# Loading the first q and k of an attention-and-experts kernel in fp32 by a hardware queue, and turning them on TensorE in fp32

## The chip, the cores and the metric

The kernel runs on one core of a Trainium2 chip. The metric is the device time of one execution in microseconds (us). The kernel before takes 1054.22 us, the median of 3 runs (1053.27 to 1054.75).

## The reference, cut to what matters

There are two parts. The first is a linear attention over 8 batches, 8 heads, 576 positions and 64 channels; its features are exponentials of a small projection, scaled by a row maximum. The second is a dense mixture of 8 experts over its output, weighted by an iterated normalisation of the routing table.

```python
def phi(x):                                   # x is q or k, per batch and head
    proj = np.einsum('bhsd,df->bhsf', x, w_phi)
    proj = proj - np.max(np.abs(proj), axis=-1, keepdims=True)
    return np.concatenate([np.exp(proj), np.exp(-proj)], axis=-1)
q_p, k_p = phi(q), phi(k)
kv = np.einsum('bhsf,bhsd->bhfd', k_p, v)     # then num / den, and out is x of the experts
...
logits = x @ w_gate                           # 4608 x 512 @ 512 x 8
...                                           # 8 normalisations of rows and columns
for e in range(8):
    out += P[:, e:e+1] * (np.maximum(x @ w1[e], 0.0) @ w2[e])
```

## The kernel before

The attention goes by pairs of heads: pair i is heads 2p and 2p+1 of batch i // 4, with p = i % 4, so there are 32 pairs (0 to 31). 512 of a head's 576 positions are the main part; the 64 that are left of all heads are the "rests", one block a batch. Matmuls of expert 0 are mixed into the attention to fill TensorE. Every operation is put in a list, and a scheduler in the program, with its own estimates of durations, fixes each engine's order when the kernel is built. On the chip each engine works in that order: an operation that has to wait holds up all that stand behind it on its engine.

The parts that the change touches (cut):

```python
def load_qk(b, hh, nh, t, r=()):              # q and k of nh heads: GpSimd queue, fp32 to bf16 on the way
    ...
    for x, src in ((1, k), (0, q)):
        dma("POOL", nh << 17, 230, lambda x=x, src=src: nc.gpsimd.dma_start(
            out=t["qk"]()[:, x, o:o + nh],
            in_=src[b, hh:hh + nh, 0:SM].rearrange("h (p j) d -> p h (j d)", j=NJ)),
            r, [(t["qk"], x, i) for i in keys])

def pair_a(b, pr, t):                         # for batches 0 and 1: TensorE turns q and k
    ...
    if b < 2:
        for x in (1, 0):
            ptr = new("P1")
            for c in range(4):
                pe(128, lambda x=x, c=c, ptr=ptr: nc.tensor.transpose(
                    bf(ptr)[:, c * 128:(c + 1) * 128],
                    t["qk"]()[:, x, h0 + c // 2, (c % 2) * 128:(c % 2) * 128 + 128],
                    ident), [(t["qk"], x, h0 // 2), "ident"], [ptr])
            dve(256, lambda x=x, ptr=ptr: nc.vector.tensor_copy(   # PSUM to SBUF, VectorE
                out=t["T"]()[:, x, 2 * h0:2 * h0 + 4, :].rearrange("p a b -> p (a b)"),
                in_=bf(ptr)[:, 0:512]), [ptr], [(t["T"], x, h0 // 2)])
    ...                                       # projections, maxima, exponentials;
    # then GpSimd multiplies v by the exponentials of the maxima ("the v product")

# start of the program
load_qk(0, 0, 2, halves[0, 0])                # pair 0
...                                           # w_phi on the SyncE queue
load_v(0, 0, 2, halves[0, 0])
pool(300, lambda: make_identity(nc, ident), w=["ident"])
...
load_rests(0, 1)                              # rests of batch 0: 4 issues on GpSimd's queue
load_qk(0, 2, 2, halves[0, 0])                # pair 1
load_v(0, 2, 2, halves[0, 0])
load_qk(0, 4, 4, halves[0, 1])                # pairs 2 and 3
load_v(0, 4, 4, halves[0, 1])
...
dma("POOL", 1 << 14, 50, lambda: nc.gpsimd.dma_start(      # gate weights, cast on the way
    out=wgate, in_=moe_w_gate.rearrange("(c p) e -> p c e", p=128)), w=["wgate"])

def stage_a(i):                               # for each pair, as it is put in the list
    b, pr = i // 4, i % 4
    st[i] = pair_a(b, pr, halves[b, pr // 2])
    if pr == 0:
        rs[b] = rest_a(b, rests[b])
    gt = [("max", 0, i - 1)] if i >= 1 else []             # loads of the next batch wait for this
    if b + 1 < B and pr in (0, 2):
        ...
        load_qk(b + 1, 2 * pr, 4, t, gt)
        load_v(b + 1, 2 * pr, 4, t, gt)
        if b + 1 >= 2:
            turn_qk(t)                        # from batch 2 on the DMA engines turn q and k
    ...
```

`acc` are the fp32 accumulators of the experts (five tiles of 128 x 4 x 512), idle in the first two batches.

## Time and profile before

| | before |
|---|---|
| time, median of 3 | 1054.22 us |
| span in the profile | 1054.0 us |
| TensorE busy | 1022.4 us, 97% |
| TensorE idle in the first 80 us | 20.2 us |
| VectorE, ScalarE, GpSimd busy | 824.6, 707.8, 475.4 us |

The first view is the profile's page: busy time and number of instructions of each engine, then the busy tenths of the span in 40 slices of 26 us (PEclk is TensorE's granted clock), then the DMA queues (packets, MB, share of the engines' time).

```profile
span 1054.0 us, 24517 instructions
...
PE 1022.4 (97%) x9512; PEld 841.3 (80%) x9512; DVE 824.6 (78%) x1634; ACT 707.8 (67%) x1560; POOL 475.4 (45%) x551
...
PE   5889999999899999999999999999999999999998
...
PEclk9899999999999999999999999999999999999999
...
q1 hardware_dynamic: 65040, 63.78, 22.3%
q0 software_dynamic: 40080, 26.23, 18.2%
...
```

TensorE (PE) is full from the fourth slice on, so only its first three slices, about 80 us, have anything to give. Of the two DMA queues, q0 is GpSimd's, which casts on the way; q1 is the hardware queue.

The next view cuts the start into stretches. After the bounds and length of a stretch stand, for each engine, the busy us and the number of instructions, then TensorE's granted clock, the DMA share and the rate.

```profile
...
core 0: us, PE busy (x) PEld busy (x) DVE busy (x) ACT busy (x) POOL busy (x), PEclk, DMA share, GB/s
0.00:5.00 5.00, 0.43 (x4) 0.35 (x4) 2.57 (x8) 1.28 (x1) 3.86 (x11) 1.00 0.49 99
5.00:10.00 5.00, 3.67 (x16) 1.42 (x14) 3.33 (x6) 2.66 (x8) 5.00 (x8) 1.00 1.35 251
10.00:15.00 5.00, 3.16 (x20) 2.23 (x21) 1.93 (x4) 2.94 (x9) 3.15 (x6) 1.00 1.52 174
15.00:20.00 5.00, 3.67 (x30) 2.31 (x29) 4.26 (x10) 5.00 (x16) 4.76 (x10) 1.00 0.86 103
20.00:25.00 5.00, 3.58 (x70) 2.90 (x70) 2.71 (x8) 1.56 (x4) 4.92 (x10) 1.00 0.26 46
25.00:30.00 5.00, 4.21 (x28) 2.56 (x26) 4.87 (x15) 4.46 (x11) 2.04 (x6) 0.57 1.34 214
...
```

Adding TensorE's busy time of the stretches up to 80 us gives 59.8 us, hence 20.2 us idle. GpSimd (POOL) is busy 4.76 and 4.92 us of 5 at 15 to 25 us. The clock of 0.57 in the last row shown is half speed for most of that stretch.

TensorE's list of waits (what was waited for, then us in total, times, longest) names two loads:

```profile
...
PE P_144 L457 <- DMA qk<-in_k_dram: 4.6, 1, 4.6
PE P_214 L395 <- DMA qk_r<-in_q_dram: 2.4, 1, 2.4
...
```

And this is the chain of waits that ended last, in order of time (start, duration, what):

```profile
...
1.26 0.48 POOL qk L324
...
3.57 1.79 POOL qk_r L367 x3
5.36 6.26 DMA qk_r<-in_q_dram
...
11.75 0.60 PE P_214 L395 x4
...
18.37 0.26 POOL vrd_88 L440
...
18.85 0.60 POOL vrd_89 L440
...
```

The rests' loads (qk_r) are issued by GpSimd from 3.57 us on and hold TensorE until 11.75 us; pair 1 stands behind them. At 18.37 to 20.5 us the chain is GpSimd's own products.

### The profile page before, as it was taken

What the parts mean: (1) busy time and instruction counts of PE and PEld (TensorE: products, weight loads), DVE (VectorE), ACT (ScalarE), POOL (GpSimd) and SP (SyncE); (2) the same over time, 40 slices, a digit from 0 to 9 for tenths busy, and PEclk for the clock granted to TensorE, in tenths of its full rate; (3) what the DMA queues carried; (4) which work ended last, traced back from release to release, by engine and by line L of the source; (5) the groups of instructions that cost most, each with busy time, mean ns of one, the idle gap of its engine ahead of it and who ended that gap; (6) DMA issues with size and microseconds to landing.
All of it is one profiled execution on the core that took longest, in us unless ns stands there. A gap on an engine that the chain in (4) does not pass through costs nothing.

```text
span 1054.0 us, 24517 instructions
## 1 busy us (share of the span) xinstructions
PE 1022.4 (97%) x9512; PEld 841.3 (80%) x9512; DVE 824.6 (78%) x1634; ACT 707.8 (67%) x1560; POOL 475.4 (45%) x551
## 2 busy tenths in 40 slices
PE   5889999999899999999999999999999999999998
PEld 3546666654588888888888888888888888888886
DVE  6889988988867787778877787778777877777775
ACT  5789989954896656666666666665666666666663
POOL 8776755510044344334444444444333544434442
PEclk9899999999999999999999999999999999999999
DMA  9998886914511133113411341116111521114333
GB/s 143 141 187 133 136 142 121 159 47 164 101 41 47 48 89 81 41 51 81 89 43 41 76 86 42 49 46 127 41 41 51 111 61 42 41 41 128 114 131 120
DMA packets 105236, 91.57 MB, mean 87 GB/s; under 512 B 45344, under 2 KB 80288, under 8 KB 105120
## 3 DMA queue, kind: packets, MB, share of 16 engines
q1 hardware_dynamic: 65040, 63.78, 22.3%
q0 software_dynamic: 40080, 26.23, 18.2%
q8 instruction: 74, 1.21, 0.5%
q14 instruction: 42, 0.34, 0.1%
HBM read 94.98 MB, written 14.16 MB: 104 GB/s over the span
## 4 chain that ended last, share of the span: by engine, by line
PE 89%; ACT 4%; DVE 3%; DMA 2%; POOL 1%; issue 1%; DVEq 0%; ACTq 0%; POOLq 0%
DVE m L376 1%; DMA qkT<-qk 1%; ACT U L1027 1%; DMA qk_r<-in_q_dram 1%; DVE xb L590 0%; PE P_13550 L999 0%; PE P_12438 L999 0%; PE P_8591 L999 0%; PE P_15513 L999 0%; PE P_14556 L999 0%; PE P_14095 L999 0%; PE P_13743 L999 0%; PE P_13392 L999 0%; PE P_13188 L999 0%; PE P_12788 L999 0%
## 5 line engine op out<-in xcount | busy, mean ns | idle before, releaser
L999 PEld LDWEIGHTS <-S 128*128 128x128 bf16 x1984 | 194.1, 98 | 22.9 <-issue 0.5
L999 PEld LDWEIGHTS <-T 128*128 128x128 bf16 x1512 | 147.9, 98 | 20.4 <-issue 3.2
L999 PEld LDWEIGHTS <-hT 128*128 128x128 bf16 x1488 | 145.6, 98 | 16.9
L907 DVE TENSOR_TENSOR S<-hT 128x1024 bf16<-128x1024 bf16 x124 | 80.3, 684 | 0.0
L1155 POOL TENSOR_TENSOR acc_77<-acc_77,V 128x512 f32<-128x512 f32 x28 | 36.3, 1308 | 54.6 <-ACT V L1152 54.5
L1155 POOL TENSOR_TENSOR acc_78<-acc_78,V 128x512 f32<-128x512 f32 x28 | 37.4, 1349 | 49.0 <-ACT V L1152 48.9
L1155 POOL TENSOR_TENSOR acc_81<-acc_81,V 128x512 f32<-128x512 f32 x28 | 35.6, 1276 | 51.0 <-ACT V L1152 50.5
L1155 POOL TENSOR_TENSOR acc_4738<-acc_4738,V 128x512 f32<-128x512 f32 x28 | 35.5, 1274 | 51.1 <-ACT V L1152 50.5
L1155 POOL TENSOR_TENSOR acc_4740<-acc_4740,V 128x512 f32<-128x512 f32 x28 | 35.2, 1268 | 51.3 <-ACT V L1152 51.2
L1155 POOL TENSOR_TENSOR acc_80<-acc_80,V 128x512 f32<-128x512 f32 x28 | 35.4, 1269 | 49.9 <-ACT V L1152 49.3
L1155 POOL TENSOR_TENSOR acc_4737<-acc_4737,V 128x512 f32<-128x512 f32 x28 | 35.6, 1277 | 49.0 <-ACT V L1152 48.4
L1155 POOL TENSOR_TENSOR acc_79<-acc_79,V 128x512 f32<-128x512 f32 x28 | 35.8, 1289 | 48.1 <-ACT V L1152 47.6
L384 PEld LDWEIGHTS <-hT 128*128 128x128 bf16 x320 | 30.7, 101 | 26.6 <-issue 2.2
L1155 POOL TENSOR_TENSOR acc_4739<-acc_4739,V 128x512 f32<-128x512 f32 x24 | 30.4, 1273 | 37.3 <-ACT V L1152 36.9
L384 PEld LDWEIGHTS <-w_449 128*128 128x128 bf16 x288 | 26.1, 98 | 24.0 <-issue 2.9
L907 DVE TENSOR_TENSOR S<-S,hT 128x1024 bf16<-128x1024 bf16 x62 | 42.5, 685 | 0.8
L907 DVE TENSOR_TENSOR S<-hT,S 128x1024 bf16<-128x1024 bf16 x62 | 42.3, 682 | 0.0
L384 PEld LDWEIGHTS <-qkT 128*128 128x128 bf16 x256 | 24.4, 102 | 20.6 <-DVE xb_r L595 4.4
L999 PEld LDWEIGHTS <-w_3831 128*128 128x128 bf16 x288 | 28.2, 98 | 4.2 <-issue 0.7
L999 PEld LDWEIGHTS <-w_13099 128*128 128x128 bf16 x288 | 28.2, 98 | 3.3
L999 PEld LDWEIGHTS <-w_11515 128*128 128x128 bf16 x288 | 28.2, 98 | 3.3
L999 PEld LDWEIGHTS <-w_5153 128*128 128x128 bf16 x288 | 28.2, 98 | 3.3
(4017 smaller groups left out, 3296.2 us busy)
## 6 DMA issues: line engine op xcount, KB each, us to landing
v_m<-in_v_dram SPq DMA_DIRECT2D x15, 512.0 KB, 5.4
qk<-in_k_dram POOLq DMA_DIRECT2D x15, 256.0 KB, 5.1
qk<-in_q_dram POOLq DMA_DIRECT2D x15, 256.0 KB, 5.8
X<-xd_98 SPq DMA_DIRECT2D x7, 256.0 KB, 2.6
X<-xd_99 SPq DMA_DIRECT2D x7, 256.0 KB, 2.7
X<-xd_100 SPq DMA_DIRECT2D x7, 256.0 KB, 2.7
X<-xd_101 SPq DMA_DIRECT2D x7, 256.0 KB, 3.1
X<-xd_102 SPq DMA_DIRECT2D x7, 256.0 KB, 2.6
```

The source lines that it names most:

```text
L376: dve(el, lambda: nc.vector.tensor_reduce(out=dst(), in_=src(), axis=AX.X, op=ALU.max, apply_absolute_value=True), r, w)
L384: nc.tensor.matmul(out_, lhsT=lhsT, rhs=rhs, start=start, stop=stop)
L907: lambda: f.tensor_tensor(out=out_(), in0=x(), in1=y(), op=op), r, w, **kw)
L999: pe(256, lambda i=i, k=k, z=z: nc.tensor.matmul(bank()[:, 256 * i:256 * i + 256], lhsT=lhs(k, i), rhs=rhs(k), start=first and z, stop=k = ...
L1027: act(512, lambda: nc.scalar.copy(out=u[fp][n]().rearrange("p a b -> p (a b)"), in_=x[fp]()), [x[fp]], [u[fp][n]])
L1155: pool(670, lambda: nc.gpsimd.tensor_tensor(out=acc[g][:, 2 * i:2 * i + 2, 256 * j:256 * j + 256], in0=acc[g][:, 2 * i:2 * i + 2, 256 * j: ...
```

## The change

Its intent: take the loads of q, k and rests of batches 0 and 1 and of the gate weights off GpSimd's queue, whose issues take GpSimd 0.6 to 0.85 us each, and start pairs 0 and 1 sooner. On the hardware queue they are loaded without a cast, so q and k land in fp32, in the idle accumulators. TensorE turns them in fp32. VectorE copies the turned k and ScalarE the turned q to bf16. The loads of batch 0's rests go behind those of pair 1. The gate weights land in fp32 and ScalarE casts them. Two more things move: the two loads of w_phi (the weights of the projection) go from SyncE's queue to ScalarE's, and the identity matrix for the turns is made in fp32 and cast to bf16 by ScalarE. As the list of operations is new, the scheduler also fixes a new order. The diff, cut to its core (the rest is dead code taken out, which leaves the operations as they were):

```diff
 def load_qk(...):
+        if b < 2:
+            g = t["f"]
+            for x, src in ((1, k), (0, q)):
+                i = 2 * x + o // 2
+                dma("SP", nh << 17, 320, lambda x=x, src=src, i=i: nc.sync.dma_start(
+                    out=acc[g][:, i:i + nh // 2].rearrange("p a (h c) -> p (a h) c", h=2),
+                    in_=src[b, hh:hh + nh, 0:SM].rearrange("h (p j) d -> p h (j d)", j=NJ)),
+                    r, [("acc", g, 2 * x + n) for n in keys])
+            return
 ...                                        # load_rests: the same, into acc[0]; rest_a: fp32 turns
 def pair_a(...):
-                    pe(128, lambda x=x, c=c, ptr=ptr: nc.tensor.transpose(
-                        bf(ptr)[:, c * 128:(c + 1) * 128],
-                        t["qk"]()[:, x, h0 + c // 2, (c % 2) * 128:(c % 2) * 128 + 128],
-                        ident), [(t["qk"], x, h0 // 2), "ident"], [ptr])
-                dve(256, ...)
+                    pe(128, lambda c=c, i=i, ptr=ptr: nc.tensor.transpose(
+                        ptr()[:, c * 128:(c + 1) * 128], acc[g][:, i, c * 128:c * 128 + 128],
+                        identf), [("acc", g, i), "identf"], [ptr])
+                if x:
+                    dve(512, lambda x=x, ptr=ptr: nc.vector.tensor_copy(...
+                else:
+                    act(512, lambda x=x, ptr=ptr: nc.scalar.copy(...
 ...                                        # w_phi's two loads: nc.sync to nc.scalar
-    pool(300, lambda: make_identity(nc, ident), w=["ident"])
+    pool(300, lambda: make_identity(nc, identf), w=["identf"])
+    act(128, lambda: nc.scalar.copy(out=ident, in_=identf), ["identf"], ["ident"])
 ...
+    load_qk(0, 2, 2, halves[0, 0])
     load_rests(0, 1)
-    load_qk(0, 2, 2, halves[0, 0])
 ...
-    dma("POOL", 1 << 14, 50, lambda: nc.gpsimd.dma_start(
-        out=wgate, in_=moe_w_gate.rearrange("(c p) e -> p c e", p=128)), w=["wgate"])
+    dma("SP", 1 << 14, 50, lambda: nc.sync.dma_start(
+        out=wgate_f, in_=moe_w_gate.rearrange("(c p) e -> p c e", p=128)), w=["wgate_f"])
+    act(32, lambda: nc.scalar.copy(out=wgate, in_=wgate_f), ["wgate_f"], ["wgate"])
```

## The prediction

> **What bounds the kernel now.** The page gives a span of 1054.0 us with TensorE busy 97%: from about 80 us on it is TensorE-bound. The change touches only the first two batches, so it can gain only what TensorE loses in the first 80 us. The table by stretches shows TensorE idle there for 20.2 us, partly at a reduced clock (0.57 and 0.75 at 25-35 us). Three causes:
> - The start. In the list of waits TensorE waits 4.6 us for the first k and 2.4 us for the first rests, behind which pair 1 stands (its turn starts at 12.1 us). DMA share is over 1 at 5-15 us, at only 174-251 GB/s.
> - GpSimd. It issues 19 loads of q, k, rests and gate weights, 0.62 to 0.85 us each, about 14 us, between its products. It is busy 4.8 to 4.9 us of each 5 at 15-25 us; the chain of waits runs through it at 18.4-22.9 us, with VectorE idle (2.7 of 5 busy).
> - VectorE. It is full (4.8 to 5.0 of 5) at 25-45 us, which sets about 6.4 us a pair.
>
> **Removed, added, moved.**
> - Loads: the GpSimd queue loses 19 issues. The first k issues at about 0.75 instead of 1.26 us and lands about 3.8 instead of 4.57 us (256 KB on the hardware queue took 3.6 us at the median). Pair 1, queued before the rests, should be ready at 7 to 8.5 us instead of 12. Products on GpSimd start 3 to 5 us earlier.
> - TensorE: 72 transposes become fp32. The trace has fp32 weight loads (routing): 190 ns against 98 for bf16. The Trainium skill, "TensorE: Matmul & The Clock Gate" (Weight-path perf modes), says fast weight load is off for FP32; the trace agrees in direction. I take one pass per transpose, about 0.8 us per group of four instead of 0.22 to 0.43: 18 groups, about +8 us of TensorE, mostly where it idles; perhaps 1.5 us of it in latency.
> - VectorE: 16 copies at 0.41 us (0.33 apart) become 8 of fp32, about 0.69 us (0.60 apart; measured on the accumulator copies). The rests' two grow. Sum: about zero. ScalarE takes the 8 q copies, about 0.5 us each: +4 us where it is 75% busy.
> - Batches 2 and 3 find free q/k slots.
>
> **On the critical path.** Start and GpSimd relief give 5 to 7 us at pair 2 (its scalars at 29.5 us, I expect 23 to 25). VectorE, ScalarE and slower turns give back 1 to 3 us by pair 7 (61.5 us, I expect 56 to 59). That shift should remain to the end. Net 4.5 us.
>
> **Predicted:** 1049.5 us, 80% range 1044.5 to 1054.5. Chances: faster by over 2% 0.01, within 2% 0.97, slower by over 2% 0.02.
>
> **What would show it.** First turn at 3.5-4.2 us; pair 1's before 9 us; no GpSimd issue of q/k before batch 2; fp32 weight loads near 190 ns, one matmul per 128x128 turn; VectorE's fp32 copy near 0.69 us; pair 7's scalars at 56-59 us; routing's first matmul (235.6 us) earlier by 3 to 6 us; length from there unchanged.
>
> **What would make it wrong.** fp32 turns in several passes (over 1.5 us a group): TensorE would bind in 10-60 us and eat the gain. SyncE's queue is in order: a load waiting for a v buffer could hold k and q behind it. Batch 1 loads may delay rests or second-half loads. A new static order could place expert 0's work worse. Upside: a warm clock earlier.

## The result and the profile after

| | before | after |
|---|---|---|
| time, median of 4 runs each | 1053.74 us | 1052.68 us |
| lowest and highest | 1051.75, 1054.75 | 1052.07, 1053.40 |
| ratio of after to before | | 0.9993, interval 0.9978 to 1.0008 |
| span in the profile | 1054.0 us | 1051.5 us |
| TensorE idle in the first 80 us | 20.2 us | 18.8 us |

Every ratio here is the mean time of one kernel's runs over that of the other's of the same rounds, so not quite the ratio of the medians beside it; the interval is a 95% one. Executions over 1.5% slower than the fastest of the same kernel are left out of the means. The forecast was a gain of 4.5 us and the medians differ by 1.1 us. The execution of before that was profiled took 1056.06 us, longer than all four timed ones; that of after, 1053.40 us, is one of the timed. Where the text gives a difference in us for an experiment, it is 1 minus the ratio, times 1054.4 us.

The page of after, the same lines:

```profile
span 1051.5 us, 24540 instructions
...
PE 1021.8 (97%) x9512; PEld 843.4 (80%) x9512; DVE 825.1 (78%) x1626; ACT 711.6 (68%) x1570; POOL 462.3 (44%) x532
...
PE   6789999999899999999999999999999999999998
...
PEclk9999999999999999999999999999999999999999
...
q1 hardware_dynamic: 71840, 68.45, 24.2%
q0 software_dynamic: 33120, 23.86, 16.5%
...
```

The start in stretches:

```profile
...
core 0: us, PE busy (x) PEld busy (x) DVE busy (x) ACT busy (x) POOL busy (x), PEclk, DMA share, GB/s
0.00:5.00 5.00, 1.26 (x6) 1.16 (x7) 2.63 (x8) 1.58 (x2) 0.70 (x6) 1.00 0.61 178
5.00:10.00 5.00, 4.82 (x26) 3.51 (x24) 3.94 (x7) 3.67 (x10) 0.37 (x1) 1.00 0.98 234
10.00:15.00 5.00, 3.12 (x22) 1.73 (x21) 4.82 (x9) 5.00 (x16) 2.99 (x8) 1.00 1.03 320
15.00:20.00 5.00, 3.19 (x38) 2.86 (x38) 1.82 (x4) 3.20 (x10) 3.90 (x9) 1.00 1.17 268
20.00:25.00 5.00, 4.14 (x57) 3.27 (x57) 3.17 (x10) 4.01 (x10) 2.49 (x6) 1.00 1.03 228
25.00:30.00 5.00, 3.42 (x33) 2.00 (x33) 5.00 (x13) 4.53 (x13) 1.36 (x3) 1.00 1.03 205
...
```

GpSimd is relieved, as meant (0.37 us busy at 5 to 10 us, and below full at 15 to 25). The DMA rate at 10 to 20 us rises from 174 and 103 to 320 and 268 GB/s. Part of this is only the type: the same q or k of four heads counts 256 KB when it lands in bf16 and 512 KB in fp32. But TensorE at 10 to 20 us is no busier than before, and VectorE falls to 1.82 us of 5 at 15 to 20 us. Something holds these engines. TensorE's list of waits up to 82 us says for which loads TensorE stands:

```profile
...
PE P L484 <- DMA acc<-in_k_dram: 5.5, 2, 3.7
...
PE P L484 <- DMA acc<-in_q_dram: 0.8, 1, 0.8
...
```

The same list for ScalarE has a load that it did not wait for before:

```profile
...
ACT wgate L770 <- DMA wgate_f<-in_moe_w_gate_dram: 1.8, 1, 1.8
...
```

And the chain of waits:

```profile
...
9.09 0.51 SPq L343
9.64 7.15 DMA wgate_f<-in_moe_w_gate_dram
16.81 0.22 ACT wgate L770
17.03 0.98 ACT k L403 x2
...
20.86 1.07 PE P L484 x8
...
```

Read it from the second line shown: the load of the gate weights, 16 KB, was the sixteenth on SyncE's queue, issued at 9.64 us, and landed 7.15 us later, at 16.79 us. ScalarE's cast of them stood, in ScalarE's fixed order, in the middle of pair 1's exponentials; so pair 1 waited for weights that the routing table needs first when batch 0 is done.

The Trainium skill, "DMA: Bandwidth & Descriptors" (Queues, rings and completion order), says that SyncE owns one row of rings and that descriptors of a ring are taken in ring order, though a later one may finish first. This trace agrees: the 16 KB landed 0.2 us after the 512 KB of v that were issued just ahead of them. Its Anatomy of one DMA gives a fit of about 2.0 us plus bytes over 436 GB/s, but for GpSimd's path, and no run here shows it for this one. A measurement is at hand instead: in the kernel without loads of q, k and rests (experiment 5) the same load took 4.5 us, so some 2.7 us of the 7.15 came with those loads.

The groups of the changed work in the first 82 us (line, engine, operation, count | busy, mean ns | idle before):

```profile
...
L484 PE MATMUL P<-identf,acc 128*128 128x128 f32 x64 | 10.2, 304 | 7.5 <-DMA acc<-in_k_dram 5.5 <-ACT qkT L492 0.9 <-DMA acc<-in_q_dram 0.8
...
L484 PEld LDWEIGHTS P<-identf,acc 128*128 128x128 f32 x64 | 8.0, 157 | 10.0 <-issue 3.9 <-DVE m L399 2.5 <-ACT em L403 2.0
...
L488 DVE CAST qkT<-P 128x512 bf16<-128x512 f32 x8 | 5.4, 689 | 4.2 <-PE P L484 4.1
...
L492 ACT CAST qkT<-P 128x512 bf16<-128x512 f32 x8 | 4.7, 608 | 3.2 <-PE P L484 3.2
...
```

And three of the turns in order of time:

```profile
...
3.74 1.94 PE L484 MATMUL P<-identf,acc 128*128 128x128 f32 x8 [3.74 <-DMA acc<-in_k_dram]
...
8.38 1.44 PE L484 MATMUL P<-identf,acc 128*128 128x128 f32 x8
...
18.37 1.06 PE L484 MATMUL P<-identf,acc 128*128 128x128 f32 x8 [1.80 <-DMA acc<-in_k_dram]
...
```

Each turn is one matmul instruction of 128 x 128. Eight of them take 1.06 us where TensorE isn't held.

Where does each pair stand? The table gives the start of a pair's first v product on GpSimd (us), read off the timelines. (The scalars of the pair, which the prediction quotes, lie about 0.3 us earlier.) "before again" and "after again" are second profiles, from the experiments below.

| | before | before again | after | after again |
|---|---|---|---|---|
| pair 0 | 9.59 | 9.58 | 9.63 | 9.59 |
| pair 1 | 20.50 | 20.17 | 18.24 | 18.38 |
| pair 2 | 29.79 | 29.27 | 28.64 | 28.74 |
| pair 3 | 34.82 | 34.17 | 34.94 | 35.03 |
| pair 7 | 61.83 | 61.18 | 60.97 | 61.96 |
| pair 8 | 69.50 | 68.84 | 66.67 | 67.67 |
| pair 15 | 114.36 | 113.46 | 111.39 | 112.37 |
| pair 31 | 221.18 | 220.28 | 218.38 | 219.33 |
| routing, first matmul | 235.80 | 233.39 | 233.00 | 232.44 |
| routing, last matmul | 268.94 | 266.60 | 266.13 | 265.65 |
| span | 1054.0 | 1051.7 | 1051.5 | 1051.0 |

The row on which most rests below is pair 2. Its lines in the timelines of before and after are:

```profile
...
29.79 1.04 POOL L501 TENSOR_TENSOR v_533<-v_m,em_521 128x512 bf16<-128x512 f32 x1 [2.96 <-ACT em_521 L380]
...
28.64 1.04 POOL L532 TENSOR_TENSOR v<-v_m,em 128x512 bf16<-128x512 f32 x1 [5.18 <-ACT em L403]
...
```

Pair 0 doesn't start earlier at all, though its first turn does (3.74 us against 4.57 us). TensorE turns k and q in one go now (1.94 us, against 0.61 us for k alone), VectorE's copy of k takes 0.69 us instead of 0.42 us, and half of w_phi's cast stands behind that copy: the first projection starts at 5.86 us, against 5.70 us before. No run tests the move of w_phi's loads by itself.

The two columns of one kernel differ by up to 2.4 us, and the granted clock shows why. In before, the clock of 0.57 in 25 to 30 us and of 0.88 in 30 to 40 us makes (0.43 x 5 + 0.12 x 10) x 2 = 6.7 us at half clock. The second profile of before has 0.83 and 0.91 there: 3.5 us. Before also has 3.4 us at half clock at routing (230.5 to 233.9 us). After has none before 120 us, but 3.4 us at routing; after again has one such window at 46 to 49 us (0.83 in a stretch of 10 us) and none at routing. The two profiles of after run together within 0.14 us up to pair 5, and 0.98 to 1.0 us apart from pair 6 on: one such window costs 1 us among the pairs. At routing it costs 1.5 us (the 0.95 us between the two, at pair 31, becomes -0.56 us). So the first two profiles, 2.5 us apart, overstate the change: before had two windows more among the pairs. The second profiles have one window each, in the pairs. They give 0.95 us at pair 31 and 0.7 us of span, which is what the timings say.

### The profile page after: what moved, and what is told of

It reads as the page before. It is cut to its first block, busy times and chain, and to the rows that moved or that the text cites. A ratio compares the mean times of both kernels' runs of the same rounds, so it can differ in the third digit from the quotient of the medians.

```text
span 1051.5 us, 24540 instructions
## 1 busy us (share of the span) xinstructions
PE 1021.8 (97%) x9512; PEld 843.4 (80%) x9512; DVE 825.1 (78%) x1626; ACT 711.6 (68%) x1570; POOL 462.3 (44%) x532
## 4 chain that ended last, share of the span: by engine, by line
PE 87%; ACT 7%; DVE 3%; issue 1%; SPq 1%; DMA 1%; POOL 0%; DVEq 0%; ACTq 0%; POOLq 0%
PE P L1022 70%; PE P L407 15%; ACT acc L1184 2%; ACT k L403 1%; ACT q L403 1%; PE P L601 1%; DVE m L399 1%; DMA wgate_f<-in_moe_w_gate_dram 1%; ACT U L1050 1%; PE P L640 0%; DVE P L613 0%; DVE xb L621 0%; ACT kr L403 0%; ACT hT L694 0%; ACT V L1174 0%
## 5 line engine op out<-in xcount | busy, mean ns | idle before, releaser
L1177 POOL TENSOR_TENSOR acc<-acc,V 128x512 f32<-128x512 f32 x248 | 317.1, 1286 | 441.6 <-ACT V L1174 438.1
L1054 DVE CUSTOM_DVE_ANT_0 hT<-P,U 128x512 bf16<-128x512 f32 x378 | 255.5, 688 | 127.1 <-ACT U L1050 77.0
L1050 ACT COPY U<-P 128x512 f32<-128x512 f32 x378 | 217.0, 588 | 125.1 <-PE P L1022 120.7
L1174 ACT ACTIVATE V<-P,P 128x256 f32<-128x256 f32 x496 | 205.5, 474 | 133.5 <-PE P L1022 131.0
L1022 PEld LDWEIGHTS <-w 128*128 128x128 bf16 x2016 | 197.2, 98 | 23.8 <-issue 0.7
L1162 DVE SCALAR_TENSOR_TENSOR acc<-P,P,acc 128x256 f32<-128x256 f32 x372 | 159.3, 478 | 55.9 <-PE P L1022 53.2
L1022 PE MATMUL P<-X,w 128*128 128x256 bf16 x1008 | 154.4, 273 | 0.5 <-ACT U L1050 0.5
L1022 PE MATMUL P<-X,T 128*128 128x256 bf16 x1008 | 148.6, 273 | 2.6 <-ACT U L1050 2.5
L1022 PE MATMUL P<-xT,w 128*128 128x256 bf16 x1008 | 150.4, 273 | 0.0
L1022 PE MATMUL P<-w,hT 128*128 128x256 bf16 x992 | 142.9, 273 | 0.0
```

What stands on the lines that cost most here:

```text
L1022: pe(256, lambda i=i, k=k, z=z: nc.tensor.matmul(bank()[:, 256 * i:256 * i + 256], lhsT=lhs(k, i), rhs=rhs(k), start=first and z, stop=k = ...
L1050: act(512, lambda: nc.scalar.copy(out=u[fp][n]().rearrange("p a b -> p (a b)"), in_=x[fp]()), [x[fp]], [u[fp][n]])
L1054: dve(500, lambda: nc.vector._custom_dve(ADD_SAT, out=out_(fp, i, j), in0=bank[fp]().rearrange("p (a b) -> p a b", a=2), in1=u[fp][n](), s ...
L1162: dve(330, lambda n=n, ts=ts: nc.vector.scalar_tensor_tensor(out=acc[g][:, ts, 256 * j:256 * j + 256], in0=bank()[:, 256 * n:256 * n + 256 ...
L1174: act(390, lambda n=n: nc.scalar.activation(out=u()[:, n, :], in_=bank()[:, 256 * n:256 * n + 256], func=ACT.Copy, bias=0.0, scale=P[:, 4 ...
L1177: pool(670, lambda: nc.gpsimd.tensor_tensor(out=acc[g][:, 2 * i:2 * i + 2, 256 * j:256 * j + 256], in0=acc[g][:, 2 * i:2 * i + 2, 256 * j: ...
```

## The experiments

Each ran in 5 rounds beside the kernel before. All results were correct unless said otherwise. "cast moved" is short for the version of the second experiment, on which some others build.

### 1. Is the small gain real, and what is the scatter?

After unedited, twice, and before unedited against itself.

> The changed kernel once more, unedited, in five rounds, to know the size of what is to be explained. If the 2.5 us between the two profiles are the gain, the ratio is about 0.9976 (-2.5 us). If the first timing is the truth, about 0.9993 (-0.7 us); the profile of before would then hold 1 to 2 us of bad luck, the 6.8 us at half clock at 25.7-32.5 us which the profile of after does not have.

> The changed kernel a third time: ratio 0.9985 to 1.0; its profile should place pair 7's first product at 60 to 63 us, depending on where half-clock stretches fall.

> The kernel before, against itself: the null. The ratio should hold 1 within 0.0013. Its profile shows whether the 6.8 us at half clock at 25.7-32.5 us, which make the profile of before 1 to 1.5 us longer than its typical run, come back at the same place (then they belong to the kernel) or not (then they are luck, and the two first profiles overstate the gain).

Measured: after 0.9997 (0.9983 to 1.0012) and 0.9989 (0.9977 to 1.0001), medians 1053.58 (of the fast runs) and 1052.96 us; before against itself 0.9999 (0.9987 to 1.0011), median 1054.1 us. With the 0.9993 above, three timings of after lie 0.3 to 1.2 us below before, 0.7 us in the mean; no single interval excludes zero.

### 2. The gate weights' cast out of the way

In the finished order only ScalarE's cast is moved, to 100 operations ahead of its first reader.

```diff
+    cast = plan.ops[-1]
...
+    def late_cast(done):
+        done.remove(cast)
+        first = min(done.index(u) for u in cast.users)
+        done.insert(first - 100, cast)
+        return done
-    plan.run(tc)
+    plan.run(tc, late_cast)      # run() applies it to the scheduler's order
```

> The changed kernel with the same order on every engine, except that ScalarE's cast of the gate weights stands about 100 operations ahead of its first reader instead of in the middle of pair 1's exponentials, where it held ScalarE 1.8 us for its load. Theory 1 (this wait eats the missing gain): pair 1's first product on GpSimd at 16.4-16.8 us instead of 18.2, and 1.3 to 2 us off the whole time against the changed kernel. Rival (VectorE and ScalarE are full at 25-40 us, or TensorE stands at loads of batch 1, so that leads of pair 1 are lost): pair 1 earlier, but pair 3 and the whole within 0.5 us of the changed kernel.

Measured: 0.9982 (0.997 to 0.9994), median 1052.13 us, 1.9 us below before. In the profile pair 2 starts at 27.87 us, and pairs 3 to 31 are all 1.06 to 1.08 us earlier than in after. Neither profile has a half-clock window among the pairs, so this shift is not the clock. A 16 KB load thus cost about 1 us, and the change brought it. (The second profile of after, up to pair 5 and so ahead of its half-clock window, gives 1.16 us at pairs 3 to 5.)

```profile
...
27.87 1.04 POOL L532 TENSOR_TENSOR v<-v_m,em 128x512 bf16<-128x512 f32 x1 [5.20 <-ACT em L403]
...
```

One part of the theory missed: pair 1 was to start at 16.4 to 16.8 us and started at 18.26 us, as in after. GpSimd's products of the rests stand ahead of it and ended at 18.18 us here, since the rests' q landed later than in the profile of after (their turn started at 10.63 us instead of 9.65). What did come earlier is ScalarE's next work for pair 1, its exponentials of q (16.90 us instead of 18.10). Before, the load on GpSimd's queue took 6.8 us to land as well, but no engine stood for it in the middle of a pair.

### 3. Only the order of the loads

In before, batch 0's rests go behind pair 1; in after, ahead of it.

```diff
+    load_qk(0, 2, 2, halves[0, 0])
     load_rests(0, 1)
-    load_qk(0, 2, 2, halves[0, 0])        # e_order_only, in before; e_rests_first is the reverse, in after
```

> The kernel before with one part of the change alone: the loads of batch 0's rests issued behind the second pair's q and k, all still in bf16 on GpSimd. If the early start of pair 1 is what gains, this gives most of it: -1 to -2 us against before. If relief of GpSimd's queue is needed, GpSimd stays full at 15-25 us and this is within 0.5 us of before.

> The changed kernel with the loads of batch 0's rests back ahead of the second pair's. If the order of loads gives the gain: +1 to +2 us against the changed kernel (pair 1 turns at about 10.5 us instead of 8.4). If not, within 0.7 us of it, since pair 1 then is held by ScalarE and the gate weights anyway.

> A version to beat both: the gate cast moved and the rests' loads ahead of the second pair's again. From e_wgate_moved (-1.9 us) and e_rests_first (-1.1 us against before, no worse than the changed kernel): 0.998 to 0.9985. If the order of the rests' loads mattered as the change assumes: 1 to 2 us worse than e_wgate_moved.

Measured: the order alone 0.9996 (0.9984 to 1.0008), median 1053.85 us. Pair 1 started at 14.48 us, 6 us earlier than before, and pair 2 at 30.67, later than before (with a half-clock window ahead of it): an early pair 1 was worth nothing by itself. GpSimd stayed full (4.61 and 4.90 us of 5 at 15 to 25 us), as the second side of that forecast said. The change with the rests first 0.999 (0.9976 to 1.0003), median 1053.67 us, no worse than after. The cast moved and the rests first: 0.9981 (0.9969 to 0.9993), median 1052.49 us, 2.0 us below before. The order of those loads earns nothing that I can measure.

### 4. Are the added turns and copies the cost? (rival: the engines are simply too full)

Each of the 64 turns of the pairs twice; each copy of turned q and k twice; q's copies on VectorE.

```diff
-                    pe(128, lambda c=c, i=i, ptr=ptr: nc.tensor.transpose(...)
+                    pe(128, lambda c=c, i=i, ptr=ptr: [nc.tensor.transpose(...) for _ in range(2)]   # e_turn_twice
-                    act(512, lambda x=x, ptr=ptr: nc.scalar.copy(...)                                # q's copies
+                    act(512, lambda x=x, ptr=ptr: [nc.scalar.copy(...) for _ in range(2)]            # e_copy_twice, and k's on VectorE
+                    dve(512, lambda x=x, ptr=ptr: nc.vector.tensor_copy(...)                         # e_q_dve
```

> The changed kernel with each of the 64 fp32 turns of pairs done twice, same order, same result: 32 groups' worth, +0.45 us of TensorE a group of four at full clock (+7 us in all in the first 41 us). If TensorE's turns are on the way of the missing gain: +3 to +6 us. If TensorE has slack there, as the prediction took it: +0.5 to +2 us (their part in latency).

> The changed kernel with each fp32 copy of turned q and k done twice: +0.6 us of VectorE and +0.5 us of ScalarE a pair for eight pairs, 4.8 and 4.0 us in all, same order, same result. If the evacuations set the pace of the first two batches (rival theory): +3.5 to +6 us. If the waits for loads do: under +2 us, as the extra work falls into them.

> The changed kernel with the eight fp32 copies of turned q on VectorE instead of ScalarE: 0.6 us each moved. If ScalarE's added 4 us hold the pairs up (it is full at 10-15 us and the chain of waits runs through it), this is faster than the changed kernel by 0.5 to 2 us; if VectorE is the bound of 25-40 us, it is slower by 1 to 4 us. The static order also changes, worth perhaps 1 us either way.

Measured: turns twice 0.9997 (0.9984 to 1.0009), 1054.36 us; copies twice 1.0006 (0.9993 to 1.0018), 1055.26 us; q's copies on VectorE 1.0015 (1.0002 to 1.0027), 1055.26 us. Against after's gain of 0.7 us that is about 0.4, 1.4 and 2.3 us lost. If a second set costs what the first does, the turns cost little and the copies over 1 us; but each of these ratios is known to 1.3 us only, so the first two losses aren't clear of noise. Only q's copies on VectorE are slower than before beyond the interval, in an order that the scheduler changed too; so giving them to ScalarE seems right. The added work takes some of the gain, but the 1.8 us together would not make up the 3.8 us that are missing, and the forecast had counted this work already.

### 5. Without the waits for loads

After's order, but q, k and rests of both batches aren't loaded; the turns read a constant tile. A second kernel leaves out batch 1's loads alone. Both compute wrong things (the comparison with the reference let them pass all the same).

```diff
+    zf = a_in.tile([128, 512], FP32, name="zf")
+    nc.vector.memset(zf, 0.03)
-                dma("SP", nh << 17, 320, lambda x=x, src=src, i=i: nc.sync.dma_start(...)
+                dma("SP", nh << 17, 320, lambda: None,
-                        ptr()[:, c * 128:(c + 1) * 128], acc[g][:, i, c * 128:c * 128 + 128],
+                        ptr()[:, c * 128:(c + 1) * 128], zf[:, c * 128:c * 128 + 128],
 ...                                       # rests alike; e_b1_free: for b == 1 only
```

> The changed kernel, every engine in its order, but the q and k of batches 0 and 1 are not loaded at all: their turns read a constant tile that is set at the start (a wrong result, on purpose). It gives the most that any faster load of them could bring in this order. If loads still set the pace (TensorE waited 1.8, 0.8 and 3.7 us for them, ScalarE 1.8 us for the gate weights behind them): -4 to -6 us against the changed kernel. If the engines' own work and the order set it from pair 1 on: -3.7 us at pair 0 at most, and -1.5 to -2.5 us in all, most of that the gate weights'.

> The changed kernel in its order, with batch 1's q, k and rests alone not loaded (their turns read a constant tile; wrong on purpose), batch 0's loads as they are. Theory 3 (batch 1's turns stand in TensorE's queue ahead of work of batch 0 and wait for loads that the plan thinks landed; and these loads slow the gate weights and batch 0): most of what all free loads gave, -2 to -3 us against the changed kernel (1050.3 to 1051.2), pair 2 at 25.5-26.5 us. Rival (batch 0's own loads hold the start): under -1.2 us.

Measured: 0.9961 (0.9948 to 0.9974), median 1049.7 us, with no loads; 0.9981 (0.9968 to 0.9994), median 1052.96 us, without batch 1's. The start in stretches, with no loads:

```profile
...
10.00:15.00 5.00, 3.73 (x30) 2.87 (x30) 5.00 (x9) 5.00 (x17) 2.81 (x8) 1.00 0.00 0
15.00:20.00 5.00, 4.44 (x67) 3.97 (x67) 3.19 (x7) 5.00 (x13) 4.86 (x11) 1.00 0.03 5
20.00:25.00 5.00, 4.04 (x45) 2.37 (x42) 5.00 (x14) 4.88 (x14) 0.98 (x3) 1.00 1.08 208
...
```

Beside the same rows of after: ScalarE is now busy 5.0, 5.0 and 4.88 us of 5 (in after 5.0, 3.2 and 4.01), VectorE 5.0, 3.19 and 5.0 (4.82, 1.82 and 3.17), and the DMA engines stand still at 10 to 20 us. Pair 2 starts at 24.87 us and pair 7 at 57.22 us; TensorE is idle for 15.5 us of the first 80. These are the places that the prediction named, and nearly its total: 4.1 us below before. So the engines can do what was predicted, with the fp32 turns, the copies and this order; what keeps them from it is the loads.

```profile
...
24.87 1.04 POOL L530 TENSOR_TENSOR v<-v_m,em 128x512 bf16<-128x512 f32 x1 [4.02 <-ACT em L401]
...
```

The gain over after, 3.4 us, lies between the two forecasts (4 to 6 us, or 1.5 to 2.5), nearer to that of the loads. This kernel takes away the gate weights' wait too: only loads of v and rests of v stand ahead of theirs. And the DMA engines have more room for what is still loaded (256 KB of expert weights took 5.3 us to land, in after 8.4 us), so it shows the weight of these loads in all, not of one wait.

Of the 3.4 us between this kernel and after, batch 1's loads make about 1.3 (2.0 us below before, against 0.7) and the gate weights about 1.1; the rest, by subtraction 1.0 us, would be batch 0's own loads: pair 0 alone starts 0.88 us earlier, at 8.75 us, and there TensorE waits for w_phi's cast next (1.5 us). That the three add up wasn't tried, and each is known to about 1.3 us only. The first two may overlap: without batch 1's loads ScalarE waited 1.1 us for the gate weights instead of 1.8. The 1.3 us also missed the forecast of 2 to 3 us, and came just above the rival's 1.2; in that profile pair 2 started at 26.96 us, not at 25.5 to 26.5.

### 6. Batch 1's turns out of the way

In the cast-moved version, turns of pair i are ordered behind the maxima of pair i - 2 (e_turn_gate), the turns of batch 1's rests behind those of pair 2 (e_gate_rest), or both (e_gate_all).

```diff
-                        identf), [("acc", g, i), "identf"], [ptr])
+                        identf), [("acc", g, i), "identf"]
+                        + [("max", 1, 4 * b + pr - 2)] * (4 * b + pr > 1), [ptr])      # e_turn_gate, e_gate_all
-                    [("acc", 0, b, h, x) for h in range(2) for x in range(2)] + ["identf"],
+                    [("acc", 0, b, h, x) for h in range(2) for x in range(2)] + ["identf"]
+                    + [("max", 1, 2)] * b,                                             # e_gate_rest, e_gate_all
```

> The changed kernel with the gate cast moved (as e_wgate_moved) and one more thing: the order places the fp32 turns of pair i not before the k maxima of pair i-2, so pair 4's turns no longer stand between the two halves of pair 0's first kv product, where TensorE waited 1.3 to 1.8 us at 16.6-18.4 us for a load of batch 1 or a PSUM bank. Theory 2 (turns of batch 1 placed too early by a plan that believes its loads land sooner hold TensorE): pair 2 at 25.5-26.5 us instead of 27.9, and 1 to 2 us off e_wgate_moved, so 1050.5 to 1051.5. Rival (VectorE and ScalarE full from 22 us on): within 0.7 us of e_wgate_moved.

> e_wgate_moved with one more thing: the turn of batch 1's rests is ordered behind the k maxima of pair 2, where nothing of batch 0 stands behind it. In e_wgate_moved TensorE waited only 0.6 us for those rests, so theory 3 gives at most 0.5 us over e_wgate_moved (1051.7 to 1052.3); more than 1 us would need another reason.

> e_turn_gate with the rests of batch 1 gated too: all turns of batch 1 now stand behind pair 2's maxima in TensorE's order; nothing else is changed. e_turn_gate let TensorE run into the rests' load instead (2.8 us at 19.4-22.2 us) and lost the clock. Theory 3: no wait of TensorE for a load of batch 1, pair 2 at 25.5-26.5 us, and 1050.3 to 1051.5 in all, -3 to -4 us against before, which is what was predicted for the change. Rival (VectorE and ScalarE full): 1052 or more, pair 2 at 27.5 us or later.

Measured: 0.999 (0.9976 to 1.0004), 1054.36 us; 0.9995 (0.9981 to 1.0008), 1053.28 us; 0.9992 (0.998 to 1.0004), 1053.35 us. None measured as well as the cast moved alone (0.9982), though the intervals overlap. With the turns gated TensorE ran into the next load instead, the rests of batch 1:

```profile
...
22.24 0.69 PE L419 MATMUL P<-identf,acc 128*128 128x128 f32 x2 [2.83 <-DMA acc<-in_q_dram]
...
```

With both gated the start came out as the theory said: pair 2 at 25.25 us, pair 5 at 43.53, 3 us ahead of the cast-moved version. Yet pair 6 started at 55.11 us, behind it, and from pair 15 on it was 1.9 to 2.1 us behind. Its profile had two half-clock windows among the pairs (clock 0.66 in 50 to 60 us), which by the costs above is about 2 us; but its five timed runs, 1053.11 to 1054.04, say that it isn't faster in general. The scheduler mixes expert 0 in differently here. How this order gives back its lead I have not settled.

### 7. Half of the change: batch 0 alone

The cast moved; batch 1 loaded by GpSimd and turned in bf16 as before. The scheduler found no order without a gate, so batch 1's turns are ordered behind the maxima of pair i - 2.

```diff
-        if b < 2:                  # in load_qk, new_half, pair_a, load_rests and rest_a
+        if b < 1:
 ...
+        if b == 1:                 # pair_a: before's bf16 turns
+                        ident), [(t["qk"], x, h0 // 2), "ident", ("max", 1, 2 + pr)], [ptr])
```

> The change with the gate weights' cast moved, but for batch 0 alone: batch 1 is loaded by GpSimd in bf16 and turned in bf16 as before (6 issues of GpSimd come back; its turns are ordered behind pair i-2). Theory (loads on the hardware queue still hold TensorE at batch 1's turns, removal of batch 1's loads was worth about 1 us): the waits of TensorE for batch 1's fp32 loads go, pair 2 starts its first v product at or below 27.9 us (cast moved: 27.87), and the time is within 1 us of the cast moved alone, -1.5 to -2.5 us against before; batch 1's half of the change is then worth nothing. Rival (GpSimd's relief by batch 1's loads is what the change earns): GpSimd is full again at 15 to 25 us, pair 2 goes back to 29 us or more and the gain to 0 to -1 us.

Measured: 1.0036 (1.0022 to 1.005), median 1057.4 us: worse than either side expected. At pair 2 the rival was right (30.97 us), though GpSimd was full only at 20 to 25 us (4.78 us of 5, and 1.78 in the 5 us before). But the greater loss came later: at pair 6 it stood at 54.42 us, 1.05 us ahead of after, and at pair 7 it was 4.64 us behind. TensorE's list of waits has a new head:

```profile
...
PE P L407 <- DMA qkT<-qk: 4.7, 1, 4.7
...
```

This is a wait for batch 2's q and k, which the DMA engines turn; it ends at 60.53 us. Batch 1 holds the two bf16 q/k slots again, and the first load of batch 2's k is issued at 38.65 us (in after at 30.90). But in before, too, batch 1 holds these slots, and there that load is issued at 32.06 us. So the slots alone don't explain it; the added gate and the new order are rivals that this run doesn't tell apart. Whether the free slots for batches 2 and 3 earn anything is not shown.

## Why the prediction was wrong

**The step that failed** is "Start and GpSimd relief give 5 to 7 us at pair 2 (its scalars at 29.5 us, I expect 23 to 25)". The runs show 0.5 to 1.2 us (28.64 and 28.74 us against 29.79 and 29.27). I took pair 2's lead from what GpSimd and the first loads had cost, as if nothing would be waited for afterwards. With loads taken away pair 2 does come 4.9 us earlier (4.4 against the second profile of before); so what was forecast was about the value of a start without waits for loads. "Products on GpSimd start 3 to 5 us earlier" failed with it: pair 0's started when they did before, pair 1's 1.8 to 2.3 us earlier. At pair 0 the added turns and copies used up the lead (it started at 10.96 us with the turns done twice, at 10.38 with the copies twice). After that, two waits took the place of the old ones:

- A new one that the text did not contain: the diff makes the gate weights a plain load at the end of the hardware queue, and their cast an operation of ScalarE. I counted only the GpSimd issue that went away. It held ScalarE for 1.8 us (0.9 in the second trace) and cost about 1 us of the total.
- Loads that all stand in one queue. The prediction listed "Batch 1 loads may delay rests or second-half loads" as a risk and gave it no time. Taking batch 1's loads away was worth about 1.3 us. In the first trace TensorE stood 1.80 us for k of batch 1, until 18.37 us. In the second profile of after the same turn started at nearly the same time, released by another engine:

```profile
...
18.44 1.06 PE L484 MATMUL P<-identf,acc 128*128 128x128 f32 x8 [1.53 <-ACT em L403]
...
```

So the named wait of 1.80 us isn't by itself the cost. Nor is it the gate weights alone that stood behind it: with the cast moved, the same turn started at 18.13 us, released by ScalarE after 1.33 us. The Trainium skill, "DMA: Bandwidth & Descriptors" (Issuing engines are not separate DMA queues), says that all loads end on the same 16 engines, whichever engine starts them, and that more issuers save only issue time. The traces are in line with this: taking the issues off GpSimd gave GpSimd its time back, but in the first 35 us the loads of k and q of four heads took 5.5 and 6.3 us to land (512 KB, the medians), in before on GpSimd's queue 4.7 and 5.6 us.

**What was right.**
- First turn at 3.74 us (3.5 to 4.2); pair 1's turn at 8.38 us (before 9); GpSimd issues no q or k before batch 2's, at 30.90 us.
- Copies: VectorE 0.69 us, as said; ScalarE 0.61 us (I had 0.5). VectorE's busy sum rose by 0.5 us, ScalarE's by 3.8 (predicted 0 and 4).
- The shift stays: from pair 15 to pair 31 the distance between the profiles of before and after is constant to 0.2 us. (But routing's first matmul came only 2.8 us earlier in the first profiles and 0.95 us in the second, where 3 to 6 were forecast.) From the last routing matmul to the end it is 785.1 us before and 785.4 after.

**What was mis-sized.** The turns: 0.8 us per group of four was forecast, +8 us in all. Eight take 1.06 us; (1.06 - 0.27) / 7 = 0.113 us apart, so a group of four adds 0.45 us. Weight loads took 157 ns in the mean, not 190, against 98 of bf16, so the direction that the prediction took from the skill's page holds. The Trainium skill, "TensorE: Matmul & The Clock Gate", Terms, mentions a transpose mode, 4 times faster for FP32; the trace shows one matmul for each turn, and no run here measures the factor.

**Nearly right for the wrong reason.** Of the give-back of 1 to 3 us by pair 7, little is there even with free loads: the lead of 4.9 us at pair 2 is 3.3 at pair 4, but 4.6 again at pair 7 (4.4, 2.7 and 4.0 against the second profile of before). In after, the lead is gone by pair 3. From there to pair 8 it swings between -1.2 and 3.3 us. Only from pair 8 on does it stay above zero (0.8 to 2.3 us between the second profiles, about 1 from pair 15 on); that another mix of expert 0 brings this gain is likely but not shown.

**The clock.** I counted on a warmer clock only as an upside. In two executions of the same kernel the half-clock windows lay at different places (in before at 25.7 to 32.5 and at 28.3 to 31.7 us, in after at routing and at 46 to 49 us). The Trainium skill, "TensorE: Matmul & The Clock Gate" (Part 1: The HAM clock gate), puts the window at 3413 ns, free-running, at half rate; windows of 3.4 us at half clock agree.

The best kernel tried is the change with the gate weights' cast moved, 0.9982, or that with the rests first too, 0.9981; both intervals exclude 1, so both beat before, by 2 us. That they beat after, by about 1 us, rests on the profile of the first (every pair from 3 on) and on ratios whose intervals overlap.

## What to carry to other kernels

When loads move to another queue, write down for each load what stands ahead of it there and which engine's fixed order will meet it; a small load at the end of a full queue, read by an operation in the middle of the hot work, can cost as much as big ones (here 16 KB about 1.1 us, all of batch 1's q, k and rests about 1.3 us). A wait that goes away is worth only the distance to the next one: forecast with the next waits in place, and test the ceiling with a kernel that doesn't load. Differences of about 1 us between single profiles need a second profile of each kernel, for TensorE's clock alone moves them by that.

## What the Trainium skill lacked or had wrong

- "TensorE: Matmul & The Clock Gate", Part 4, gives durations of bf16 transposes only. Here an fp32 turn of 128 x 128 took 1.06 us for eight (0.113 us apart), with weight loads of 157 ns in the mean.
- The same page, HAM oscillation, speaks of idle gaps over about 3.4 us, and the section after it of frequent short ones, for which it gives no cost. In before the clock fell to half at 25 to 32 us, where the longest wait of TensorE in its list after the first turn was 2.4 us, at 9 us; and in two profiles of one kernel the windows lay at different places (near 46 us or at routing), at 1 to 1.5 us each.
- "DMA: Bandwidth & Descriptors", Anatomy of one DMA: the fit of 2.0 us plus bytes over the rate doesn't say what a load pays behind others on its queue. Here 16 KB took 7.15 us behind q, k, rests and v, and 4.5 us behind v alone.
